# Lambda-mask attention with a gated feed-forward part: the first two 384-row halves computed the same way, each weight group used by both in turn

## The chip, the cores and the metric

One core of a Trainium2 chip. The metric is device microseconds (us) of one execution. Runs of the kernel before lie within 1.3% of each other (258.0 to 261.2 us, 35 runs of the fifth call). A run that is over 1.5% above the fastest of the same kernel is called slow here and left out of every ratio; medians take in all runs. A verdict is "faster" or "slower" from 2% on.

## The reference, cut to what matters

```python
# q, k, v: 4 batches, 8 heads, 768 rows, 64 columns, float32; n_global = 8, n_local = 96
scores = scale * np.matmul(q, k.transpose(0, 1, 3, 2))
rel = pos[:, None] - pos[None, :]
is_global = pos[None, :] < n_global
is_local = (rel >= 0) & (rel < n_local)
dist = np.where(is_global & ~is_local, n_local, np.abs(rel))
scores = scores - slopes[:, None, None] * dist          # one slope for each head
scores = np.where(is_global | is_local, scores, -1e9)
a = softmax(scores);  x = (a @ v), heads side by side: 3072 rows of 512
gate = np.maximum(x @ w_gate, 0.0);  val = x @ w_val    # 512 -> 1536
return (gate * val) @ w_out                             # 1536 -> 512
```

## The kernel before

Each batch is cut into two halves of 384 rows, eight in all, called half 0 to half 7. The attention of a half is made of small pieces that are laid among the feed-forward matmuls of the half before (`weave` places a piece by the share of the work done). Program order on each engine's queue is the order in which these lines are called.

The inputs of half 2 and later go this way: GpSimd casts k and q to bf16, the sync queue transposes them by DMA, and GpSimd copies the transposed keys into `kT`, whose key tiles overlap by the 8 global keys. Pieces of one half in this order:

```python
    def early_pieces(s):
        out = [(0.0, lambda p=p: piece_cast_k(s, p)) for p in range(HP)]     # GpSimd casts
        out += [(0.0, lambda n=n: piece_xk(s, n)) for n in range(NN)]        # sync: kN <- kc
        out += [(0.0, lambda p=p: piece_cast_q(s, p)) for p in range(HP)]    # GpSimd casts
        out += [(0.0, lambda n=n: piece_xq(s, n)) for n in range(NN)]        # sync: qT <- qz
        out += [(0.0, lambda p=p: piece_order(s, p)) for p in range(HP)]     # GpSimd: kT <- kN
        return out
```

v and the weights are loaded by GpSimd, cast to bf16 on the way; k and q by the sync queue. The 8 global rows of v are loaded once and copied six times within SBUF, by DMA on the sync queue:

```python
    def spread_v_globals(b, j0=1, j1=NT):
        for j in range(j0, j1):
            nc.sync.dma_start(out=v_dst(b, 0, NG, j), in_=v_dst(b, 0, NG, 0))
```

The start of the program (cut):

```python
    weave(f1_0, attention_pieces(1),                       # half 1's attention among half 0's gates and vals
          [(0.05 * h, lambda h=h: mask(h)) for h in range(H)])
    ...
    load_w(wo_sb, moe_w_out, 0, DM)                        # output weights, on GpSimd
    ...
    load_qk_after(2)
    load_v_half(2)
    weave(f1_1, spread(early_pieces(2), 0.0, 1.0))
    load_qk(3, 0, H)
    load_v_half(3)
    weave(f2_0 + f2_1, spread(attention_pieces(2), 0.0, 0.9), spread(early_pieces(3), 0.2, 0.7))
```

The softmax here doesn't subtract the row's maximum and nothing guards it: scores larger than these inputs give would overflow.

Of the kernel before, what the change touches and what calls it, by code (L numbers as in the profile page):

```python
# [8 lines left out]
FP32 = mybir.dt.float32  # L9
# [6 lines left out]
def kernel(  # L16
# [45 lines left out]
    banks_of_half[1] = [[by[1, 2], by[1, 5]], [by[1, 3], by[1, 6]], [by[1, 4]]]  # L62
    first_groups = [[by[0, 0], by[0, 1]], [by[0, 2], by[0, 3]]]

# [12 lines left out]
    first = ExitStack()  # L77
    P["es"] = first.enter_context(tc.tile_pool(name="es2", bufs=4))
    P["qk"] = first.enter_context(tc.tile_pool(name="qkps2", bufs=3, space=bass.MemoryType.PSUM))

    def other_pools():
        first.close()
        P["es"] = ctx.enter_context(tc.tile_pool(name="es", bufs=3, reuse_waits="tile"))
        P["qk"] = ctx.enter_context(tc.tile_pool(name="qkps", bufs=3, space=bass.MemoryType.PSUM,
                                                 reuse_waits="tile"))
        P["ff"] = ctx.enter_context(tc.tile_pool(name="ffps", bufs=3, space=bass.MemoryType.PSUM,
                                                 reuse_waits="tile"))
# [61 lines left out]
    def load_v_half(s):  # L149
        b, half = divmod(s, 2)  # L150
        if half == 0:
            load_v_globals(b)
            spread_v_globals(b)
        for j in range(4) if half == 0 else range(4, NT):
            load_v(b, j)
# [7 lines left out]

    def load_qk_after(s, by_pairs=False):

        qs_of[s] = stage.tile([128, H, NN * D], FP32, name="qs")
        ks_of[s] = stage.tile([128, H, NN * D], FP32, name="ks")
        step = 2 if by_pairs else H
        for t in (qs_of[s], ks_of[s]):
            nc.vector.memset(t[0:1, 0:H:step, 0:1], 0.0)  # L170
        for h in range(0, H, step):
            load_qk(s, h, h + step)
# [6 lines left out]
    nc.vector.memset(ones, 1.0)  # L179
    warm_ps = av_psum.tile([128, 512], FP32, name="av_ps")  # L180

    def warm(n):

        for _ in range(n):
            nc.tensor.matmul(warm_ps, lhsT=wo_sb[:, 0, 0:128], rhs=wo_sb[:, 0, :], start=True, stop=True)
# [43 lines left out]
    def piece_cast(s, p):  # L229
        qk = cast_pool.tile([128, 2, NN, 2, D], BF16, name="qk")  # L230
        cast_of[s, p] = qk
        for i, src in ((1, ks_of[s]), (0, qs_of[s])):
            copy = nc.gpsimd.tensor_copy
            if s == 0 and p < 3:
                copy = (nc.vector.tensor_copy, nc.scalar.copy, nc.scalar.copy)[p]
            copy(
                qk[:, i].rearrange("t n e d -> t e n d"),
                src[:, 2 * p : 2 * p + 2, :].rearrange("t e (n d) -> t e n d", n=NN))
# [20 lines left out]
    def piece_t(s, p):  # L259
# [5 lines left out]
        for i in range(2):  # L265
            for n in range(NN):
# [3 lines left out]
                                 start=(i == 0 and n == 0), stop=(i == 1 and n == NN - 1))  # L270
        if s == 0:
            nc.vector.tensor_copy(qTb[0][:, p, 0, :], tp[:, 0, :])
        else:
            qd = qTb[s % 2][:, p]
            nc.vector.tensor_copy(qd[0:64, 0, :], tp[0:64, 0, :])
            nc.vector.tensor_copy(qd[64:128, 1, :], tp[64:128, 0, :])
        put_keys(nc.vector.tensor_copy, nc.vector.tensor_copy, kt, tp[:, 1, :], half)
# [34 lines left out]

    def piece_bias(p, g):

        ps = P["qk"].tile([128, 2, 512], FP32, name="qk_ps")
        ps_of[p, g] = ps
        for e in range(2):
            c = 0
            for i, (j, a, w, m) in enumerate(first_groups[g]):
                nc.tensor.matmul(ps[:, e, c : c + NN * w], lhsT=sid[:, 2 * p + e],  # L320
                                 rhs=dd[:, 0 if j == 0 else 1, :, m : m + w],
                                 start=(i == 0), stop=False, skip_group_check=True)
                c += NN * w

    def piece_score(p, g):

        kt = kT[0][p]
        qd = qTb[0][:, p, 0, :].rearrange("d (n p) -> d n p", n=NN)
        group = first_groups[g]
        cols = sum(NN * w for _, _, w, _ in group)  # L330
        ps = ps_of[p, g]
        es = P["es"].tile([128, 2, cols], BF16, name=f"es{g}")
        c = 0
        for i, (j, a, w, m) in enumerate(group):
            for e in range(2):
# [3 lines left out]
                                 skip_group_check=True)  # L339
            es_of[0, p, j] = (es, c)  # L340
            c += NN * w
        nc.scalar.activation(es, ps[:, :, 0:cols], AF.Exp, bias=0.0, scale=scale)

# [58 lines left out]

    def piece_av_wide(p):

        s = 0
        todo = [t for group in first_groups for t in group]
        if p % 2 == 1:
            t = P["qk"].tile([128, 2, 512], FP32, name="qk_ps")
            av = [t[:, i] for i in range(2)]
        else:  # L410
            av = [av_psum.tile([128, 512], FP32, name="av_ps") for _ in range(2)]
# [19 lines left out]
    def attention_pieces(s):  # L431
        T = lambda p: [(0.34, lambda: piece_t(s, p))]
        QK = lambda p: [(0.18, lambda g=g: piece_qk(s, p, g)) for g in range(3)]
        AW = lambda p: [(0.58, lambda: piece_av_wide(p))]
        AV = lambda p: [(0.29, lambda e=e: piece_av(s, p, e)) for e in range(2)]
        C = lambda p: [(0.0, lambda: piece_cast(s, p))]
        BI = lambda p, *gs: [(0.2, lambda g=g: piece_bias(p, g)) for g in gs]
        SC = lambda p, *gs: [(0.2, lambda g=g: piece_score(p, g)) for g in gs]
        X = lambda *fs: [(0.0, f) for f in fs]
        if s == 0:  # L440
            return (C(0) + X(lambda: load_v_globals(0), lambda: load_v(0, 0)) + C(3)
                    + X(lambda: load_v(0, 1), lambda: load_v(0, 2), lambda: spread_v_globals(0, 1, 4),
                        lambda: load_v(0, 3), lambda: load_w_group(0))
                    + C(1) + T(0) + BI(0, 0, 1) + C(2) + T(1) + SC(0, 0, 1) + BI(1, 0) + SC(1, 0) + T(2)
                    + BI(1, 1) + SC(1, 1) + BI(2, 0) + T(3) + SC(2, 0) + BI(2, 1) + SC(2, 1)
                    + BI(3, 0) + SC(3, 0) + BI(3, 1) + SC(3, 1)
                    + AW(0) + X(lambda: load_qk_after(1, True)) + AW(1) + AW(2) + AW(3) + X(other_pools))
        if s == 1:
            at = lambda *ts: list(ts)
            C_ = lambda p: piece_cast(1, p)  # L450
            return ([(0.0, lambda: C_(0)), (0.0, lambda: C_(1)), (0.02, lambda: load_w_group(1)),
                     (0.04, lambda: C_(2)), (0.05, lambda: C_(3)), (0.07, lambda: load_w_group(2))]
                    + [(0.08, lambda j=j: fill_ones(nc.gpsimd, 0, j)) for j in range(NT)]
                    + [(t, lambda p=p: piece_t(1, p)) for p, t in enumerate((0.10, 0.14, 0.20, 0.26))]
                    + [(t, lambda p=p, g=g: piece_qk(1, p, g))
                       for p, ts in enumerate(((0.15, 0.18, 0.22), (0.26, 0.30, 0.34), (0.38, 0.42, 0.46),
                                               (0.54, 0.58, 0.62))) for g, t in enumerate(ts)]
                    + [(t, lambda p=p, e=e: piece_av(1, p, e))
                       for p, ts in enumerate(((0.37, 0.42), (0.52, 0.56), (0.66, 0.70), (0.81, 0.85)))
                       for e, t in enumerate(ts)])  # L460
        g = QK(3)
# [80 lines left out]
    for p in range(HP):  # L542
        nc.gpsimd.memset(qTb[1][64:128, p, 0, :].bitcast(mybir.dt.uint32), 0)
        nc.gpsimd.memset(qTb[1][0:64, p, 1, :].bitcast(mybir.dt.uint32), 0)

    f1_0, f2_0 = ffn_pieces(0)
    f1_1, f2_1 = ffn_pieces(1)
    weave(f1_0, attention_pieces(1),
          [(0.05 * h, lambda h=h: mask(h)) for h in range(H)])
    for p in range(HP):  # L550
        nc.gpsimd.memset(kT[1][p][:, 3, 32:128].bitcast(mybir.dt.uint32), 0)
        nc.gpsimd.memset(kT[1][p][:, 6, NG + 48 : 128].bitcast(mybir.dt.uint32), 0)
    nc.gpsimd.memset(vbuf[1][:, NT - 1, :].bitcast(mybir.dt.uint32), 0)
    for j in range(NT):
        fill_ones(nc.gpsimd, 1, j)
    load_w(wo_sb, moe_w_out, 0, DM)
    for i in range(2):
        nc.gpsimd.memset(qz[i].rearrange("t n p e z -> t (n p e z)").bitcast(mybir.dt.uint32), 0)
    load_qk_after(2)
    load_v_half(2)  # L560
    weave(f1_1, spread(early_pieces(2), 0.0, 1.0))
    load_qk(3, 0, H)
    load_v_half(3)
    weave(f2_0 + f2_1, spread(attention_pieces(2), 0.0, 0.9), spread(early_pieces(3), 0.2, 0.7))

# [45 lines left out]
```

## Time and profile before

| | before |
|---|---|
| time, median of 4 runs | 259.96 us (259.52 to 260.48) |
| profiled span | 258.3 us, granted clock 0.985 |
| TensorE busy | 238.5 us (92%) |
| TensorE idle from 17.45 to 90.44 us | 10.4 us (5.6 + 2.1 + 2.7 in the prediction's stretches) |

The prediction shows the page and TensorE's waits. What it did not look at closely, and what the result turned on, is the order on two DMA queues. The sync queue's timeline (start, length of issuing, line, what, count) and the piece of the chain of waits in which the last of these three transposes lands:

```profile
63.17 3.94 SPq L295 DMA_TRANSPOSE qT<-qz  x3
```

```profile
65.80 2.84 DMA qT<-qz
```

And GpSimd's:

```profile
37.42 1.04 POOL L158 DMA_DIRECT2D wo_sb<-in_moe_w_out_dram  x1
```

Half 2's three query transposes take 3.94 us to issue and the last lands 2.84 us after its issue began; TensorE waits 0.79 us for them:

```profile
68.77 0.53 PE L355 MATMUL qk_ps<-qT,kT 128*128 128x432 bf16 x2 [0.79 <-DMA qT<-qz]
```

The output weights (1536 KB, 12.9 us from issue to landing) are issued at 37.42 and are in the chip by about 50, long before those transposes. That order is an accident of where half 2's loads stood.

### The profile page before, as it was taken

The page shows a single profiled execution, that of the slowest core. Times are in us where ns is not written, and L with a number is a line of the kernel's source. Part 1 is how long each engine was busy: PE and PEld are TensorE (multiplying, and loading weights), DVE is VectorE, ACT ScalarE, POOL GpSimd, SP SyncE. Part 2 cuts the span into 40 slices and gives each one's busy share as a digit, 9 for nine tenths or more (in the row PEclk, how much of TensorE's full clock was granted, in tenths as well). Part 3 has the DMA queues.
Part 4 walks back from the last instruction along what each step waited for, and adds up shares of the span by engine and source line. Part 5 has one row for each costly group of instructions (what it writes and reads, how often), then busy time and mean ns, then how long its engine had stood idle before and what let it go on. Part 6 is the DMA issues. An engine that isn't in the chain of part 4 may idle for free.

```text
span 258.3 us, 4682 instructions
## 1 busy us (share of the span) xinstructions
PE 238.5 (92%) x1623; PEld 139.5 (54%) x1623; DVE 131.7 (51%) x333; ACT 159.3 (62%) x325; POOL 97.7 (38%) x244
## 2 busy tenths in 40 slices
PE   6754988999898899999999999999999999999994
PEld 2541645556454466655665566655665566556541
DVE  3521788644354467634675276625773457614410
ACT  5772689633376677756875577747774677643311
POOL 7791899015864706800644235600640000000000
PEclk9997799999999999999999999999999999999999
DMA  6999999994899993855681995927591200021012
GB/s 176 115 142 226 207 208 173 176 219 116 212 276 185 173 291 91 141 71 156 190 141 26 196 255 119 107 88 207 133 119 53 81 3 1 0 84 41 0 43 82
DMA packets 82695, 34.36 MB, mean 133 GB/s; under 512 B 58608, under 2 KB 79600, under 8 KB 82672
## 3 DMA queue, kind: packets, MB, share of 16 engines
q1 hardware_dynamic: 50816, 26.16, 38.8%
q0 software_dynamic: 31856, 7.91, 31.6%
q8 instruction: 13, 0.21, 0.3%
q14 instruction: 10, 0.08, 0.1%
HBM read 28.38 MB, written 6.29 MB: 134 GB/s over the span
## 4 chain that ended last, share of the span: by engine, by line
PE 65%; DMA 15%; SPq 5%; DVE 5%; ACT 5%; POOL 2%; issue 2%; DVEq 0%; ACTq 0%; POOLq 0%
PE ff_ps L497 21%; PE ff_ps L488 18%; PE ff_ps L478 17%; DMA qs<-in_q_dram 8%; PE av_ps L383 5%; PE qk_ps L355 4%; DVE xT L400 3%; DMA wv<-in_moe_w_val_dram 3%; SPq L291 2%; SPq L122 2%; DMA vbuf<-in_v_dram 2%; ACT rcp L397 1%; ACT lnd L392 1%; DVE ht L490 1%; DMA kN<-kc 1%
## 5 line engine op out<-in xcount | busy, mean ns | idle before, releaser
L488 PE MATMUL ff_ps<-xT,wv 128*128 128x384 bf16 x384 | 79.4, 330 | 4.6 <-DMA wv<-in_moe_w_val_dram 3.8
L478 PE MATMUL ff_ps<-xT,wg 128*128 128x384 bf16 x384 | 79.0, 328 | 3.7 <-DMA wg<-in_moe_w_gate_dram 2.9
L481 ACT ACTIVATE grelu<-ff_ps 128x384 bf16<-128x384 f32 x96 | 47.0, 490 | 38.2 <-DVE ht L490 18.2
L490 DVE TENSOR_TENSOR ht<-ff_ps,grelu 128x384 bf16<-128x384 f32 x96 | 53.1, 555 | 29.5 <-PE ff_ps L488 25.1
L497 PE MATMUL ff_ps<-wo_sb,ht 128*128 128x512 bf16 x288 | 67.3, 379 | 0.0
L400 DVE TENSOR_TENSOR xT<-av_ps,rcp 64x384 bf16<-64x384 f32 x56 | 31.1, 556 | 46.5 <-ACT rcp L397 42.1
L358 ACT ACTIVATE es<-qk_ps 128x432 bf16<-128x432 f32 (+2 forms) x84 | 44.2, 532 | 14.1 <-PE qk_ps L355 12.6
L367 DVE TENSOR_TENSOR es<-es,m_all 128x432 bf16<-128x432 bf16 (+6 forms) x128 | 39.2, 337 | 26.9 <-ACT es L358 26.3
L488 PEld LDWEIGHTS <-wv 128*128 128x128 bf16 x384 | 36.5, 98 | 27.8 <-DMA wv<-in_moe_w_val_dram 4.3
L478 PEld LDWEIGHTS <-wg 128*128 128x128 bf16 x384 | 36.5, 98 | 26.5 <-DMA wg<-in_moe_w_gate_dram 3.3
L497 PEld LDWEIGHTS <-ht 128*128 128x128 bf16 x288 | 27.0, 97 | 28.1
L280 POOL CAST kc<-ks 128x384 bf16<-128x384 f32 x24 | 12.1, 549 | 60.7 <-DMA ks<-in_k_dram 60.7
L392 ACT ACTIVATE lnd<-av_ps 64x384 f32<-64x384 f32 x56 | 27.2, 485 | 12.8 <-PE av_ps L383 12.0
L355 PE MATMUL qk_ps<-qT,kT 128*128 128x432 bf16 (+6 forms) x128 | 28.8, 285 | 0.9 <-DMA qT<-qz 0.8
L502 ACT COPY osb<-ff_ps 128x512 f32<-128x512 f32 x24 | 14.1, 586 | 24.2 <-PE ff_ps L497 21.7
L383 PEld LDWEIGHTS <-vbuf 128*128 128x128 bf16 x256 | 21.0, 98 | 11.0 <-issue 2.7
L383 PE MATMUL av_ps<-es,vbuf 128*128 128x216 bf16 (+5 forms) x256 | 25.1, 225 | 1.7 <-DVE xT L400 1.7
L141 POOL DMA_DIRECT2D vbuf<-in_v_dram x28 | 24.4, 882 | 0.5 <-issue 0.4
L355 PEld LDWEIGHTS <-kT 128*128 128x128 bf16 x128 | 12.4, 98 | 10.7 <-issue 2.3
L288 POOL CAST qz<-qs 128x192 bf16<-128x192 f32 x48 | 14.4, 351 | 4.0 <-DMA qs<-in_q_dram 4.0
L397 ACT ACTIVATE rcp<-lnd 128x384 f32<-128x384 f32 x28 | 14.6, 522 | 0.9
L251 POOL COPY kT<-kN 128x360 bf16<-128x360 bf16 x12 | 6.6, 551 | 5.9 <-DMA kN<-kc 5.9
(75 smaller groups left out, 108.2 us busy)
## 6 DMA issues: line engine op xcount, KB each, us to landing
out_dram<-osb SPq DMA_DIRECT2D x24, 256.0 KB
ks<-in_k_dram SPq DMA_DIRECT2D x6, 768.0 KB
qs<-in_q_dram SPq DMA_DIRECT2D x6, 768.0 KB
vbuf<-in_v_dram POOLq DMA_DIRECT2D x24, 120.0 KB, 4.8
ks<-in_k_dram SPq DMA_DIRECT2D x8, 192.0 KB
qs<-in_q_dram SPq DMA_DIRECT2D x8, 192.0 KB
wg<-in_moe_w_gate_dram POOLq DMA_DIRECT2D x3, 512.0 KB, 7.4
wv<-in_moe_w_val_dram POOLq DMA_DIRECT2D x3, 512.0 KB, 10.2
```

Source lines behind the costliest of these rows:

```text
L141: nc.gpsimd.dma_start(out=v_dst(b, NG + r0, NG + r0 + n, j), in_=v[b, :, KT * j + r0 : KT * j + r0 + n, :].rearrange("h p d -> p h d"))
L355: nc.tensor.matmul(ps[:, c : c + n_], lhsT=kt[:, j, :], rhs=qd[:, :, :, a : a + w], start=True, stop=True)
L358: nc.scalar.activation(es[:, 0:cols], ps[:, 0:cols], AF.Exp, bias=0.0, scale=scale)
L367: nc.vector.tensor_mul(e4, e4, mk)
L383: nc.tensor.matmul(av3[:, :, a : a + w], lhsT=vb[:, j, z0 : z0 + 128], rhs=es[:, c : c + NN * w].rearrange("k (n p) -> k n p", n=NN), star ...
L392: nc.scalar.activation(ln[o0 : o0 + 64], av[d0 : d0 + 64, 0:QH], AF.Ln, bias=0.0, scale=1.0)
L400: nc.vector.tensor_tensor(xT_of[s][r, p, :], av_of[s, p, e_][r, 0:QH], rc[r], op=ALU.mult)
L478: nc.tensor.matmul(psg[:, 0:QH], lhsT=w_of(wg, dc, fc), rhs=xT[:, dc, :], start=(dc == 0), stop=(dc == N_DC - 1))
L481: nc.scalar.activation(gr, psg[:, 0:QH], AF.Relu, bias=0.0, scale=1.0)
L488: nc.tensor.matmul(psv[:, 0:QH], lhsT=w_of(wv, dc, fc), rhs=xT[:, dc, :], start=(dc == 0), stop=(dc == N_DC - 1))
L490: nc.vector.tensor_tensor(ht[:, fc, :], psv[:, 0:QH], st["gr"], op=ALU.mult)
L497: nc.tensor.matmul(ps2, lhsT=ht[:, fc, n * 128 : (n + 1) * 128], rhs=wo_sb[:, fc, :], start=(fc == 0), stop=(fc == N_FC - 1))
```

## The change

Its intent: half 1 gets its distance bias from TensorE (a matmul into the scores' buffer) and its scores in row halves, as half 0 has them, so that VectorE is spared the masks; half 1's attention comes in one burst after weight group 0 of half 0; then each of the three groups of gate and val weights is used by half 0 and half 1 in turn, which gives the later groups more time to arrive. The casts of half 0's last pair of heads go from GpSimd to VectorE, so that v and the weights are issued earlier; eight matmuls without use ("warm") bridge a gap at the first gate. Half 2's inputs are fetched some 20 us earlier. The diff, cut to its core:

```diff
-    weave(f1_0, attention_pieces(1),
-          [(0.05 * h, lambda h=h: mask(h)) for h in range(H)])
+    weave(f1_0[G[0]], spread(attention_pieces(1), 0.75, 3.0))
+    other_pools()
+    load_w_group(2)
+    load_qk_after(2, nc.gpsimd)
 ...
+    load_v_globals(1)
+    e2 = early_pieces(2)
+    for _, f in e2[:-HP]:               # casts and transposes of half 2
+        f()
     load_w(wo_sb, moe_w_out, 0, DM)     # now BEHIND half 2's casts on GpSimd
-    load_qk_after(2)
+    for _, f in e2[-HP:]:               # key copies of half 2
+        f()
+    spread_v_globals(1)
     load_v_half(2)
-    weave(f1_1, spread(early_pieces(2), 0.0, 1.0))
-    load_qk(3, 0, H)
-    load_v_half(3)
-    weave(f2_0 + f2_1, spread(attention_pieces(2), 0.0, 0.9), spread(early_pieces(3), 0.2, 0.7))
+    weave(f1_1[G[0]] + f1_0[G[1]] + f1_1[G[1]],
+          [(0.1 + 0.1 * h, lambda h=h: mask(h)) for h in range(H)])
+    weave(f1_0[G[2]] + f1_1[G[2]] + f2_0 + f2_1,
+          [(0.4, lambda: load_qk(3, 0, H)), (0.4, lambda: load_v_half(3))],
+          spread(attention_pieces(2), 0.15, 0.8), spread(early_pieces(3), 0.5, 0.9),
+          [(0.02 * j, lambda j=j: fill_ones(nc.vector, 0, j)) for j in range(NT)])
 ... (in half 0)
-                    + AW(0) + X(lambda: load_qk_after(1, True)) + AW(1) + AW(2) + AW(3) + X(other_pools))
+                    + AW(0) + X(lambda: load_qk_after(1, nc.vector, True)) + AW(1) + AW(2) + AW(3) + X(second_pools, lambda: warm(8)))
```

Nothing in the stated intent asks for the output weights to move. The line kept its place among its neighbours, and half 2's casts and transposes moved ahead of it.

## The prediction

> **What bounds the kernel now.** I read first the busy shares and the 40 slices of the page, for the engine that is full and the stretch in which it is not.
>
> ```profile
> PE 238.5 (92%) x1623; PEld 139.5 (54%) x1623; DVE 131.7 (51%) x333; ACT 159.3 (62%) x325; POOL 97.7 (38%) x244
> PE   6754988999898899999999999999999999999994
> ...
> DMA  6999999994899993855681995927591200021012
> ```
>
> TensorE is full from the fifteenth slice (90 us) to the end. Then I cut the trace into stretches and read the busy time of each engine in each (columns: stretch, length, then PE, PEld, DVE, ACT and POOL with their counts, granted clock, DMA share, GB/s).
>
> ```profile
> 17.45:29.10 11.65, 6.06 (x30) 3.48 (x31) 3.94 (x10) 4.04 (x9) 5.66 (x15) 0.71 1.29 215
> 29.10:51.58 22.48, 20.36 (x157) 12.70 (x155) 18.17 (x54) 18.67 (x40) 15.87 (x37) 1.00 1.35 186
> 51.58:90.44 38.86, 36.18 (x218) 19.91 (x218) 16.95 (x39) 20.12 (x42) 21.92 (x56) 1.00 1.03 197
> 90.44:231.16 140.72, 140.10 (x934) 82.95 (x932) 79.19 (x192) 96.40 (x194) 39.77 (x107) 1.00 0.56 117
> ```
>
> After 90.44 TensorE idles 0.6 us in 141. The change leaves that code alone, so its whole worth lies before 90 us: 5.6 us idle in the first stretch, 2.1 in the second, 2.7 in the third. The clock adds to it. One-microsecond stretches show 0.50 from 22 to 28.6 us, and from 23.87 on TensorE is busy all the time, so some 4.9 us of work ran at half speed: 2.4 us lost. Together 12.8 us could be had at the very most. What ended the idle times stands in TensorE's timeline (start, length, line, what, count, idle before it and its releaser).
>
> ```profile
> 20.34 0.82 PE L478 MATMUL ff_ps<-xT,wg 128*128 128x384 bf16 x4 [2.90 <-DMA wg<-in_moe_w_gate_dram]
> 23.87 1.46 PE L488 MATMUL ff_ps<-xT,wv 128*128 128x384 bf16 x4 [2.70 <-DMA wv<-in_moe_w_val_dram]
> ...
> 35.95 0.82 PE L488 MATMUL ff_ps<-xT,wv 128*128 128x384 bf16 x4 [1.05 <-DMA wv<-in_moe_w_val_dram]
> ...
> 40.37 0.47 PE L383 MATMUL av_ps<-es,vbuf 128*128 128x72 bf16 x5 [0.74 <-DVE xT L400]
> ```
>
> So the feed-forward part starts on the weights' DMA, and four matmuls of 384 columns took 1.46 us at half clock against 0.82. Why the weights are late, the GpSimd timeline and two windows of one microsecond show.
>
> ```profile
> 8.34 0.51 POOL L236 CAST qk<-ks 128x384 bf16<-128x384 f32 x1 [1.12 <-DMA ks<-in_k_dram]
> 9.11 0.51 POOL L236 CAST qk<-qs 128x384 bf16<-128x384 f32 x1 [0.27 <-DMA qs<-in_q_dram]
> 9.56 2.70 POOL L141 DMA_DIRECT2D vbuf<-in_v_dram  x3
> 12.26 0.79 POOL L158 DMA_DIRECT2D wg<-in_moe_w_gate_dram  x1
> ```
>
> ```profile
> 9.00:10.00 1.00, 1.00 (x18) 0.69 (x18) 0.23 (x1) 1.00 (x3) 0.89 (x2) 1.00 0.66 42
> 10.00:11.00 1.00, 0.89 (x14) 0.71 (x10) 1.00 (x5) 0.57 (x2) 1.00 (x2) 1.00 0.04 7
> ```
>
> GpSimd waits for a slice of k, casts it, and only then issues v and the weights; meanwhile the DMA engines run dry (7 GB/s).
>
> **What the Trainium skill says.** "TensorE: Matmul & The Clock Gate", part 1: the clock falls to half after an idle window of about 3.4 us and returns after a busy one, the window running free. The trace agrees in length: half clock lasted 6.6 us, about two windows; but the window before the fall was not quite empty, it held 0.65 us of matmuls. The same page, "Back-to-back issue gap": N/2.4 + 2.5 ns, so 162.5 ns for 384 columns; the chain of waits after 90 us steps by 0.65 us for four, which agrees. "TensorEngine Tiling (Array Packing)", "Key Properties": different tiles run in parallel, but changing the mode drains the array. In the first half's attention four row-half matmuls of 216 columns took 0.29 us (12.65 to 12.94), where two side by side twice would be 0.18: parallel, with a toll.
>
> **The change, part by part.** I call the 384-row halves 0, 1, 2; one feed-forward item is four matmuls, 0.65 us; a half has 24 such items plus 7.8 us for its output (36 matmuls at 0.216).
>
> Earlier loads. The two casts move to VectorE (0.36 us each), so three v loads and the first weights are issued 2.4 us sooner (wg at 9.9 instead of 12.26) into the dry stretch. The attention of half 0 is held by ScalarE and would gain only 1 us (last normalised tile at 18.8 instead of 19.8). First gate at about 18.9, first val at 21.4 instead of 23.87: minus 2.4 us.
>
> Eight warming matmuls (1.7 us at full clock) fill about 16.7 to 18.4. The longest gap then is near 1.8 us before the first val, where before there were 2.9 and 2.7 us. If that holds the clock: minus 2.4 us. I give this 60%, as the window's phase is chance.
>
> Half 1's attention is no longer spread among 24 items but comes as one burst after group 0 of half 0. On TensorE a pair of heads costs: transpose 0.34; bias 1392 columns in 10 matmuls, about 0.80 (0.75 in half 0 for 1200); scores in row halves 0.53; sums and values in column halves 0.66. That is 2.33, for four pairs 9.3 us. Before it was 20.36 - 85 x 0.1625 = 6.5 in the second stretch plus 0.6 for two transposes, 7.1. Plus 2.2 us of TensorE work. The masks' multiplications (20 at 0.2 to 0.4 us) and half the normalising on VectorE go; these lay beside TensorE.
>
> What paces the burst is ScalarE. From the groups by shape: 864 columns 890 ns, 336 columns 446 ns, hence 0.84 ns a column; 816 and 576 columns cost 0.85 and 0.65. Four pairs: 4 x 1.50 + 4 x (0.48 logarithm + 0.52 reciprocal) = 10.0 us in a row. First exponential at about 27.7 (group 0 done at 26.5, transposes and VectorE's copies 1.2 us), and the emission order (two score buffers, two output buffers, each freed by the step before) adds about 1 us of bubbles: half 1's last tile at 39. TensorE idles 3.1 us in the burst (11.7 less 8.6), against the 2.1 of the second stretch before. Plus 1.0.
>
> Only two feed-forward buffers during group 0: a val waits for the multiply of the val before, some 0.15 us three times. Plus 0.4.
>
> Groups in turn. After the burst 24 items run bare on loaded weights (group 1 is needed at 44, not at 36), then 16 items and both outputs, 26 us, take half 2's attention from 0.15 to 0.8. Its inputs are fetched from about 30 us instead of 52, so the waits for q and the late normalisation (0.79, 0.97, 0.16, 0.77 us) go. What remains is the transposed q of half 3, queued behind outputs on the sync queue: I leave 0.7. Minus 2.0.
>
> Sum: -2.4 - 2.4 + 2.2 + 1.0 + 0.4 - 2.0 = -3.2 us with the clock held, -0.8 without. The last stages are the same. Working out the burst step by step gave about -4, so 256.2 to 257 with the clock held.
>
> **The rivals.** (1) The burst eats the gain: TensorE gets 2.2 us more work and nothing to fill ScalarE's 10 us with. If each hand-over costs 0.2 us more, half 1 ends at 41 to 42 and the time is 259 to 260. For it: ScalarE was 5.0 of 5.0 us busy from 30 to 35 with less in a row. Against: VectorE loses its masks, which had held it full there. (2) The DMA was saturated anyway: from 20 to 28 us it moved 190 to 260 GB/s, so earlier issue might only reorder. Then the first val stays at 23, the clock falls, and the time is about 259. Against: the dry stretch at 10 us is free capacity. (3) Better than I think: the burst's idle time shrinks to nothing, the weights come 3 us earlier, no wait remains before 90 us; then some 252. (4) A fetch that now comes too late (output weights, issued after half 2's casts) stops the outputs: 261 or more. It has some 20 us of slack, so this is unlikely.
>
> **Range and chances.** Between the sum with clock held (257.0) and the step-by-step working (256.0), with some weight on (3) because the constants look tuned, and on (1) and (2): 256.3. Range 252.8 to 259.6. Faster by over 2% needs under 255.0, that is, nearly all parts working: 0.30. Slower by over 2% needs (4): 0.03.
>
> **What would show it right or wrong.** The granted clock at 1.00 from 18 to 30 us; wg and wv read first at about 19 and 21.4; no second wait for weights; half 1's first gate of group 0 at about 38 to 39; TensorE idle about 3 us in the burst with ScalarE nearly full; under 1 us idle between the burst and the third half's first gate at about 85 to 86. It is wrong if the clock falls all the same, if wv is not read before 23, or if the burst lasts beyond 41.

## The result, and the profile after

| | before | after |
|---|---|---|
| median (range) | 259.96 us (259.52 to 260.48), 4 runs | 273.40 us (270.04 to 274.98), 4 runs |
| fast runs | all four, mean 259.98 | 272.63 and 270.04, mean 271.34 |
| profiled span, clock | 258.3 us, 0.985 | 270.7 us, 0.967 |

The ratio of the fast runs is 1.044, 95% interval 1.035 to 1.053: slower. Ratios here are the mean time of one kernel's fast runs over that of the other's of the same rounds, so not quite the ratio of the medians quoted. The loss to be explained is that of the fast runs, 11.4 us; the median is 13.4 only because two of four runs are slow. The prediction was 256.3 us; it was wrong, in direction too.

The page of the changed kernel (busy tenths of TensorE and granted clock, 40 slices of 6.8 us each):

```profile
PE   6969979990999959999999999999999999999994
...
PEclk9979999997699986999999999999999999999999
```

The tenth slice of TensorE shows 0: around 61 to 68 us it does nothing at all. In that slice and the next the clock drops, and there is a second, smaller dent of both five slices on. TensorE's timeline names the two waits (in brackets the idle time before the instruction, and what ended it):

```profile
68.30 0.52 PE L358 MATMUL qk_ps<-qT,kT 128*128 128x432 bf16 x1 [8.05 <-DMA qT<-qz]
...
100.07 0.56 PE L358 MATMUL qk_ps<-qT,kT 128*128 128x144 bf16 x2 [3.25 <-DMA qT<-qz]
```

These are the first scores of half 2 and of half 3, each waiting for its transposed q. Each wait is also paid a second time: the clock falls to 0.50, and work runs at half speed until it returns. Windows of one microsecond show 0.50 from 65.0 to 71.8 us (3.5 us of it with matmuls, so about 1.75 lost) and from 99.1 to 105.9 (5.85 us of it busy, about 2.9 lost); a window with a mean of 0.55 has fallen for nine tenths of its length. Three of the windows (length, busy time of PE, PEld, DVE, ACT and POOL, clock, DMA share, GB/s):

```profile
66.00:67.00 1.00, 0.00 (x0) 0.00 (x0) 0.00 (x0) 0.00 (x0) 0.00 (x0) 0.50 1.70 156
...
71.00:72.00 1.00, 1.00 (x7) 0.49 (x6) 0.38 (x1) 0.25 (x2) 0.00 (x0) 0.60 1.15 347
...
99.00:100.00 1.00, 0.00 (x0) 0.00 (x0) 0.00 (x0) 0.00 (x0) 0.00 (x0) 0.55 1.53 281
```

From 66 to 67 us no engine works, and the DMA moves 156 GB/s. 8.05 + 1.75 + 3.25 + 2.9 = 16.0 us; less the waits of about 2.7 us that the kernel before had in that stretch and the 0.4 us by which the changed kernel was ahead at half 1's first val (reckoned at the end), that is 12.9, against a difference of the two profiled spans of 12.4. So the loss is in these two places, within half a microsecond, and elsewhere the change is worth little.

Why does q come late? The sync queue, to be held against the one line of before:

```profile
47.99 13.90 SPq L298 DMA_TRANSPOSE qT<-qz  x3
61.99 4.37 SPq L146 DMA_DIRECT2D vbuf<-vbuf  x6
66.40 0.45 SPq L131 DMA_DIRECT2D ks<-in_k_dram  x1
...
81.19 3.81 SPq L496 DMA_DIRECT2D out_dram<-osb  x2
...
91.59 3.99 SPq L298 DMA_TRANSPOSE qT<-qz  x3
```

The same three transposes took 13.90 us to issue in place of 3.94, and held up everything behind them: value rows, and half 3's keys and queries, loaded at 66.4. Half 3's own query transposes then stand behind outputs of half 0 and half 1 and are issued at 91.59. In the chain of waits half 2's last transpose lands 10.23 us after its issue, not 2.84, and half 3's last 5.65 us after:

```profile
57.94 10.23 DMA qT<-qz
...
94.28 5.65 DMA qT<-qz
```

Half 3's last transpose has half 4's value loads beside it (issued by GpSimd from 93.23 us on). At 2.84 us it would have landed by 97.1, and of the second wait some 0.4 us would be left (an estimate from these lines). So that wait may be made by the place on the queue or by the company at that place.

And GpSimd, shortly before and during this:

```profile
46.71 1.03 POOL L167 DMA_DIRECT2D wo_sb<-in_moe_w_out_dram  x1
...
55.22 6.11 POOL L150 DMA_DIRECT2D vbuf<-in_v_dram  x7
```

Two suspects share the DMA engines with half 2's transposes: the output weights (1536 KB, issued at 46.71, landing after 15.2 us, at about 62) and seven value loads of 120 KB. The value loads can't have begun the delay: at the pace of before, 5.47 us from the first issue to the last landing (63.17 to 68.64), the transposes would have landed by 53.5, before the first value load was issued. They can have drawn it out, as the last transpose lands 6 us after the output weights.

The head of the program changed too:

```profile
17.01 0.20 PE L420 MATMUL av_ps<-es,vbuf 128*64 128x24 bf16 x2 [2.32 <-DMA vbuf<-vbuf]
...
22.14 0.81 PE L471 MATMUL ff_ps<-xT,wg 128*128 128x384 bf16 x4
22.79 0.81 PE L481 MATMUL ff_ps<-xT,wv 128*128 128x384 bf16 x4
```

The first half's values wait 2.32 us for the copied global rows, and the first gate runs at 22.14, later than before (20.34); but the first val runs at 22.79, not 23.87, and at full clock. One trace says little here, though: nine kernels of this study (the changed one, `e1_wo_first` to `e5_half3_first`, `e9_order_warm`, `e11_two_moves`, `e13_keys_after_scores`) have the same code up to this point, and in their traces the first val runs anywhere from 20.84 to 24.82 us (the middle one 22.88) and half 1's first gate from 37.67 to 41.65 (39.14 to 41.65 within the first call). What makes this spread is not known. The two traces of the old head have the first val at 23.87 and 24.04.

### The profile page after: what moved, and what is told of

The parts are those of the page before. It is cut to its first block, busy times and chain, and to the rows that moved or that the text cites. A ratio compares the mean times of both kernels' runs of the same rounds, so it can differ in the third digit from the quotient of the medians.

```text
span 270.7 us, 4853 instructions
## 1 busy us (share of the span) xinstructions
PE 248.3 (92%) x1731; PEld 146.3 (54%) x1731; DVE 124.3 (46%) x312; ACT 158.0 (58%) x317; POOL 92.7 (34%) x229
## 4 chain that ended last, share of the span: by engine, by line
PE 71%; DMA 10%; SPq 6%; ACT 4%; DVE 4%; POOL 2%; issue 2%; POOLq 0%; DVEq 0%; ACTq 0%
PE ff_ps L481 20%; PE ff_ps L490 19%; PE ff_ps L471 19%; DMA qT<-qz 6%; PE qk_ps L358 5%; PE av_ps L386 4%; SPq L298 4%; DMA vbuf<-vbuf 2%; DVE xT L403 2%; DMA vbuf<-in_v_dram 1%; DVE ht L483 1%; ACT es L345 1%; SPq L294 1%; DMA kN<-kc 1%; PE qk_ps L420 1%
## 5 line engine op out<-in xcount | busy, mean ns | idle before, releaser
L361 ACT ACTIVATE es<-qk_ps 128x432 bf16<-128x432 f32 (+2 forms) x72 | 37.9, 529 | 23.9 <-PE qk_ps L358 22.3
L370 DVE TENSOR_TENSOR es<-es,m_all 128x432 bf16<-128x432 bf16 (+5 forms) x108 | 32.4, 328 | 41.2 <-ACT es L361 40.7
L403 DVE TENSOR_TENSOR xT<-av_ps,rcp 64x384 bf16<-64x384 f32 x48 | 26.7, 555 | 45.3 <-ACT rcp L400 40.7
L358 PE MATMUL qk_ps<-qT,kT 128*128 128x432 bf16 (+5 forms) x108 | 26.0, 298 | 11.3 <-DMA qT<-qz 11.3
L283 POOL CAST kc<-ks 128x384 bf16<-128x384 f32 x24 | 12.4, 557 | 68.3 <-DMA ks<-in_k_dram 68.3
L395 ACT ACTIVATE lnd<-av_ps 64x384 f32<-64x384 f32 x48 | 23.3, 485 | 10.5 <-PE av_ps L386 9.8
L386 PEld LDWEIGHTS <-vbuf 128*128 128x128 bf16 x216 | 18.1, 98 | 7.8 <-issue 0.5
L358 PEld LDWEIGHTS <-kT 128*128 128x128 bf16 x108 | 10.8, 101 | 20.1 <-issue 13.1
L386 PE MATMUL av_ps<-es,vbuf 128*128 128x216 bf16 (+4 forms) x216 | 21.3, 226 | 0.2 <-DVE xT L403 0.2
L345 ACT ACTIVATE es<-qk_ps 128x864 bf16<-128x864 f32 (+3 forms) x16 | 10.7, 706 | 4.2 <-PE qk_ps L340 4.2
L400 ACT ACTIVATE rcp<-lnd 128x384 f32<-128x384 f32 x24 | 12.5, 523 | 0.8
```

What stands on the lines that cost most here:

```text
L358: nc.tensor.matmul(ps[:, c : c + n_], lhsT=kt[:, j, :], rhs=qd[:, :, :, a : a + w], start=True, stop=True)
L361: nc.scalar.activation(es[:, 0:cols], ps[:, 0:cols], AF.Exp, bias=0.0, scale=scale)
L370: nc.vector.tensor_mul(e4, e4, mk)
L386: nc.tensor.matmul(av3[:, :, a : a + w], lhsT=vb[:, j, z0 : z0 + 128], rhs=es[:, c : c + NN * w].rearrange("k (n p) -> k n p", n=NN), star ...
L395: nc.scalar.activation(ln[o0 : o0 + 64], av[d0 : d0 + 64, 0:QH], AF.Ln, bias=0.0, scale=1.0)
L403: nc.vector.tensor_tensor(xT_of[s][r, p, :], av_of[s, p, e_][r, 0:QH], rc[r], op=ALU.mult)
```

## The experiments

Fourteen kernels, in the order in which they ran, as diffs against the changed kernel ("after") if nothing else is said. All gave correct results.

**First call: which load slows the transposes?** Before: 259.69 us in the same call.

`e1_wo_first`, the output weights' load put ahead of half 2's casts on GpSimd:

```diff
+    load_w(wo_sb, moe_w_out, 0, DM)
     load_v_globals(1)
     e2 = early_pieces(2)
     for _, f in e2[:-HP]:
         f()
-    load_w(wo_sb, moe_w_out, 0, DM)
```

> The changed kernel with one line moved: the output weights' load is issued by GpSimd before half 2's casts (at about 36 us) instead of after them (46.7 us). Theory A: the three transposes of q took 13.9 us to issue and the last landed 10.2 us after its issue because this load shared the DMA engines with them. Then they issue in about 4 us, land within 3 us, the 8.05 us stall of TensorE before half 2's first scores falls to under 1 us, the clock stays full from 60 to 72 us, and the second stall (3.25 us at 97) shrinks as half 3's loads are no longer late: about 257 to 260 us. Theory B: the seven v loads of small packets issued at 55 us made it. Then the stall stays near 8 us and the time near 272.

Measured: 261.19 us (260.43 to 265.73, one of four slow), ratio to before 1.006 [1.000, 1.012], a little above the 257 to 260 expected. Its sync queue:

```profile
53.80 4.24 SPq L298 DMA_TRANSPOSE qT<-qz  x3
```

And its TensorE:

```profile
90.28 0.36 PE L358 MATMUL qk_ps<-qT,kT 128*128 128x144 bf16 x2 [3.34 <-DMA qT<-qz]
```

One moved line brought back some 10 us (mean of the fast runs 260.94, from 271.34): issuing takes 4.24 us again and the wait at half 2 is gone. q itself arrives later, as its load now shares with the output weights (GpSimd's casts of q wait 6.17 us, until 51.37), and still it is in time. The second wait, at half 3, stays; that its loads were no longer late did not help it.

`e2_v_first`, half 2's value loads put ahead, the output weights left: 

```diff
     load_v_globals(1)
+    load_v_half(2)
 ...
     spread_v_globals(1)
-    load_v_half(2)
```

> The changed kernel with half 2's four v loads issued before half 2's casts (about 36 us), the output weights' load left after the casts. Theory A (output weights contend): the stall before half 2's first scores stays at 5 us or more, the time at 268 or more. Theory B (v loads contend): the stall goes, 257 to 260 us. If both share it, something between, with the last transpose landing sooner than 68 us but the second one's issue still at several us.

Measured: 271.63 us, ratio 1.047 [1.042, 1.052]; waits of 8.36 and 3.18 us.

```profile
49.66 11.46 SPq L298 DMA_TRANSPOSE qT<-qz  x3
```

With half 2's four value loads out of the way the wait is as long as before (issuing 11.46 us in place of 13.90, the last landing 15.64 us after its issue), so these four don't make it. Half 3's three value loads are still issued at 55.23 us, so a share of theirs in the slow landing is not excluded; as in the changed kernel they come too late to have begun it (49.66 + 5.47 = 55.1).

`e3_both_first`, both moves at once:

> The changed kernel with both loads issued before half 2's casts, in the order of the kernel before. Under A and B alike the transposes run alone as they did in the kernel before: issue about 4 us, landing about 3 us, no stall over 1 us before half 2's first scores, 256 to 259 us. If the stall stays, neither load is its cause, and it is something that the transposes do by themselves at this place (theory C).

Measured: 266.02 us, ratio 1.024 [1.016, 1.031]. Issuing took 5.61 us, but q was cast only from 54.4 on, the first wait is 1.91 us and the second still 3.17. Too much ahead of q is no good either: the loads in front of it delay q itself. Its head also waited longer (4.4 us for the copied rows), but the moved loads are issued only at 37.8 us, so that is the spread of the head and no work of the edit.

**Second call: dose, the second wait, the warm matmuls, the earlier loads.** Before: 259.55 us.

`e4_half_wo`, one half of the output weights ahead of the casts and the other behind:

```diff
+    nc.gpsimd.dma_start(out=wo_sb[:, 0:6], in_=moe_w_out[0:768, :].rearrange("(c p) f -> p c f", p=128))
     load_v_globals(1)
 ...
-    load_w(wo_sb, moe_w_out, 0, DM)
+    nc.gpsimd.dma_start(out=wo_sb[:, 6:12], in_=moe_w_out[768:1536, :].rearrange("(c p) f -> p c f", p=128))
```

> Dose: the changed kernel with the first half of the output weights' load issued early, as in e1, and the second half left behind half 2's casts. If the transposes of q are slow because they share the DMA engines with the bytes of this load, the q transposes should take about half as long to issue as in the changed kernel (6 to 9 us instead of 13.9), the stall of TensorE before half 2's first scores should fall from 8 us to between 0 and 4 us, and the time to some 261 to 267 us. If it is the mere presence of any load behind the casts (an ordering or a semaphore), the stall stays at 7 us or more and the time near 272.

Measured: 272.97 us, ratio 1.050 [1.045, 1.055]: a miss. Half the load beside the transposes did not give half the loss. The early half delayed q (cast at 48.34 in place of 44.38), the late half was issued at 50.67 just as the transposes began, and these took 10.22 us to issue; the wait was 6.82 us. So the loss doesn't go with the load's size alone; where it lies to the transposes counts. How the two share the engines in detail stays open.

`e5_half3_first`, `e1_wo_first` and further half 3's loads and transposes ahead of half 1's outputs on the sync queue:

```diff
     load_v_globals(1)            # behind the output weights, as in e1_wo_first
+    spread_v_globals(1)
 ...
-    spread_v_globals(1)
+    load_qk(3, 0, H)
     load_v_half(2)
+    load_v_half(3)
 ...
-          [(0.4, lambda: load_qk(3, 0, H)), (0.4, lambda: load_v_half(3))],
-          spread(attention_pieces(2), 0.15, 0.8), spread(early_pieces(3), 0.5, 0.9),
+          spread(attention_pieces(2), 0.15, 0.8), spread(early_pieces(3), 0.42, 0.5),
```

> e1 with the sync queue reordered: half 2's copies of the global v rows before its transposes, half 3's q and k loads straight after them, and half 3's transposes placed between 0.42 and 0.5 of the stage, ahead of all but the first output. Theory: the second stall (3.34 us at 90 us in e1, and 3 us of half clock after it) is half 3's transposes queued behind four outputs. Then it goes, and the time falls from 261 to about 256 to 257.5, 1 to 1.5% under the kernel before. Rival: half 3's transposes are slow from half 4's v loads at the same time; then a stall of 2 us or more stays, and 259 to 260.

Measured: 268.42 us, ratio 1.032 [1.025, 1.038]. The wait at half 3 is gone. This edit moves half 3's loads too; `e11_two_moves` below moves only its casts, transposes and key copies, and the wait goes as well. But I had put the copies of the global value rows ahead of the transposes, and they wait for a load that now stands behind the output weights:

```profile
52.38 4.63 SPq L146 DMA_DIRECT2D vbuf<-vbuf  x6
...
61.13 3.95 SPq L298 DMA_TRANSPOSE qT<-qz  x3
```

The transposes are fast (3.95 us) but late, and TensorE waits 4.63 us. A wait of my own making.

`e6_no_warm`, the same without the eight warm matmuls:

```diff
-                    ... + AW(3) + X(second_pools, lambda: warm(8)))
+                    ... + AW(3) + X(second_pools))
```

> e5 without the eight warming matmuls. My prediction gave them 2.4 us at 60%. If they hold the clock, without them the feed-forward part starts at half clock and the time is 1.5 to 2.5 us over e5. If the clock comes back by the attention's matmuls alone, or the start is held by something else, the difference is under 0.7 us.

Measured: 267.54 us, ratio to before 1.029 [1.024, 1.034], nothing to tell from `e5_half3_first`. But this pair can't price the warm matmuls. In the trace without them half 1's first gate runs at 38.11 us, with them at 41.48, and half 2's first score comes at the same time all the same, for it waits for q in both:

```profile
66.74 0.34 PE L358 MATMUL qk_ps<-qT,kT 128*128 128x432 bf16 x1 [4.63 <-DMA qT<-qz]
66.76 0.52 PE L358 MATMUL qk_ps<-qT,kT 128*128 128x432 bf16 x1 [8.02 <-DMA qT<-qz]
```

(The first line is `e5_half3_first`, the second `e6_no_warm`.) Whatever the head gains or loses, this wait takes up. The clock is at 0.50 from 16.0 to 22.9 us with them and from 17.4 to 20.8 without, and at 1.00 after it until that wait.

`e7_late_loads`, `e5_half3_first` with the cast of the last pair of heads of half 0 back on GpSimd, ahead of the v and weight loads, as in the kernel before:

```diff
-            return (C(0) + X(lambda: load_v_globals(0), lambda: load_v(0, 0), lambda: load_v(0, 1),
+            return (C(0) + X(lambda: load_v_globals(0), lambda: load_v(0, 0)) + C(3) + X(lambda: load_v(0, 1),
```

> e5 with the cast of the last pair of heads of half 0 back on GpSimd ahead of three v loads and the first weights, as in the kernel before. My prediction gave the earlier issue 2.4 us. In the trace of the changed kernel half 0's values waited 2.3 us for the copies of the global v rows, which share the DMA engines with the loads now issued earlier. If the earlier issue gains what the first val shows (1.1 us), e7 is about 1 us over e5; if the copies' delay eats it, the two are within 0.5 us; if my term was right, 2 us or more.

Measured: 269.89 us, ratio 1.038 [1.032, 1.044]; the first val waits for its weights 2.05 us and runs at 23.87. The total is 1.5 us above that of `e5_half3_first`, but this does not price the head either: half 1's first gate runs at 40.71 us, earlier than the 41.48 there. The time is lost at half 2, whose query transposes are issued at 63.63 in place of 61.13; TensorE waits 7.90 us for them. What the trace does show is that TensorE's last waits at the head are here for the value loads (1.31 and 0.58 us) and not for the copied rows.

**Third call: the orders mended, and the cause tried on the kernel before.** Before: 260.34 us.

`e8_order_no_warm` and `e9_order_warm`: `e5_half3_first` with the global rows' load ahead of the output weights, and the copies between half 2's key and query transposes; without and with the warm matmuls.

```diff
     load_v_globals(1)
+    load_w(wo_sb, moe_w_out, 0, DM)
     e2 = early_pieces(2)
-    for _, f in e2[:-HP]:
+    for _, f in e2[: HP + NN]:
         f()
-    load_w(wo_sb, moe_w_out, 0, DM)
+    spread_v_globals(1)
+    for _, f in e2[HP + NN : -HP]:
+        f()
+    load_qk(3, 0, H)
     for _, f in e2[-HP:]:
         f()
-    spread_v_globals(1)
     load_v_half(2)
+    load_v_half(3)
```

> The changed kernel without the eight warm matmuls, with the output weights' load issued first of all on GpSimd after the second batch's global value rows (as in e1_wo_first), the copies of those rows on the sync queue between half 2's key and query transposes, half 3's query and key loads right behind half 2's query transposes on the sync queue, and half 3's transposes ahead of half 1's late outputs. Theory (the time of the change went into two waits for query transposes, the first made by the output weights' load running beside them, the second by their place behind other work on the sync queue; the rest of the change is worth about what was predicted): no wait of TensorE for query transposes above 1.5 us, query transposes' issue about 4 us for half 2 and half 3, first half's attention ends at about 38 us, total 253 to 257 us, 1 to 3% below the kernel before. Rival (the two halves together cost TensorE more than the removed work, or there is a third wait that the two hid): waits gone but total 260 us or more. Second rival (every ordering moves the wait: the transfers of this stretch are simply more than the queues carry in the time): a wait of 3 us or more at half 2's or half 3's scores, total 262 to 268 us.

> As e8_order_no_warm but with the eight warm matmuls kept. If the warm matmuls hold the clock, this is 1 to 3 us faster than e8_order_no_warm; if, as e6_no_warm showed, the clock comes back without them, it is 0 to 2 us slower, with the first gate 2 to 3 us later.

Measured: 263.95 us, ratio 1.014 [1.007, 1.020], and 264.09 us, ratio 1.015 [1.010, 1.019]: the range of the second rival (each order moves the wait), not of the theory. The totals with and without the warm matmuls don't differ. In the profile of `e8_order_no_warm` half 2 still waits 2.89 us for q; in that of `e9_order_warm` no wait for q above 0.2 us is left, but a new one took its place:

```profile
68.12 0.27 PE L386 MATMUL av_ps<-es,vbuf 128*128 128x216 bf16 x1 [1.78 <-DMA vbuf<-in_v_dram]
```

Three such waits for half 2's values, 3.1 us in all, with half clock from 68.6 to 75.4 us. Half 3's k and q, now issued at 58.88, run beside half 2's value loads, issued at 58.94.

`e10_before_wo_late`, the kernel *before* with its output weights' load behind half 2's query casts:

```diff
-    load_w(wo_sb, moe_w_out, 0, DM)
 ...
-    weave(f1_1, spread(early_pieces(2), 0.0, 1.0))
+    e2 = early_pieces(2)
+    e2.insert(2 * HP + NN, (0.0, lambda: load_w(wo_sb, moe_w_out, 0, DM)))
+    weave(f1_1, spread(e2, 0.0, 1.0))
```

> The kernel before with one line moved: the output weights' load is issued on GpSimd only behind half 2's query casts, where the changed kernel has it, so that it runs beside half 2's query transposes. Theory (the load beside them slows the transposes): their issue on the sync queue grows from 3.94 us to 8 us or more and their landing from 2.84 us to 5 us or more, and a wait for them of some us appears at half 2's scores; total 2 to 8 us over before. Rival (the changed kernel's stall comes from its other traffic or from its ordering, the output weights only being a part of it): issue stays below 5.5 us and the total within 1 us of before.

Measured: 274.06 us, ratio 1.050 [1.043, 1.056]. GpSimd's line, the sync queue's and the chain's:

```profile
62.05 1.05 POOL L158 DMA_DIRECT2D wo_sb<-in_moe_w_out_dram  x1
```

```profile
62.88 12.88 SPq L295 DMA_TRANSPOSE qT<-qz  x3
```

```profile
71.56 10.21 DMA qT<-qz
```

Set these beside the changed kernel's 13.90 and 10.23, and the 3.94 and 2.84 of before: in a kernel that has nothing else of the change, one moved load makes the same slow transposes. (The total, well above the 2 to 8 us expected, is not all theirs: TensorE also waits 10.15 us for the output weights themselves, and then 2.48 for q.)

**Fourth call: only what is needed.** Before: 260.07 us over all its runs.

`e11_two_moves`, `e1_wo_first` and one number pair more, so that half 3's casts and transposes stand ahead of the outputs and its loads stay where they are:

```diff
-          spread(attention_pieces(2), 0.15, 0.8), spread(early_pieces(3), 0.5, 0.9),
+          spread(attention_pieces(2), 0.15, 0.8), spread(early_pieces(3), 0.42, 0.5),
```

> e1_wo_first (the output weights' load put ahead of half 2's key and query casts, 261.2 us) with one more move and nothing else: half 3's casts and transposes at 0.42 to 0.50 of the second stretch of work in place of 0.5 to 0.9, so that they stand ahead of half 1's outputs on the sync queue. Half 3's loads stay where they are, so half 2's values aren't disturbed as in e8_order_no_warm and e9_order_warm. Theory (two waits for query transposes were the whole loss, and each has one cause: the load beside them, the place in the queue): both waits are gone, so the 3.3 us of TensorE's idle time and about 1.7 us of low clock that e1_wo_first still had go too, total 255 to 258 us, 1 to 2% below the kernel before. Rival (the stretch holds more transfers than its time carries, so each removed wait comes back in another place, as in e9_order_warm): some other wait of 2 us or more between 60 and 100 us, total 260 us or more.

Measured: 261.11 us median of 22 runs, five of them slow; ratio 1.003 [1.001, 1.005]. Both old waits are nearly gone (1.75 us at half 2, none at half 3), and a third appeared, as the rival had said; the trace explains it:

```profile
80.24 0.22 PE L358 MATMUL qk_ps<-qT,kT 128*128 128x48 bf16 x1 [2.36 <-POOL kT L264]
```

This is the last score of half 2. It reads key tile 3, whose tail half 3's keys fill. With the pieces moved up, GpSimd's copies for half 3 come *before* this score in program order, so it must wait for them.

`e12_two_moves_no_warm`, the same without the warm matmuls:

> e11_two_moves without the eight warm matmuls. By e6_no_warm against e5_half3_first and e8_order_no_warm against e9_order_warm: within 1 us of e11_two_moves, if anything 0.5 us less, the clock being 0.50 for one window near 17 to 21 us and 1.00 after it with or without them.

Measured: 264.63 us median of 6 runs, from 259.94 to 266.48; only two count as fast (mean 261.27, against 260.87 for the fast runs of `e11_two_moves`), so there is no interval. Its trace is the one hint that the warm matmuls may do something. The first val with and without them:

```profile
20.84 0.81 PE L481 MATMUL ff_ps<-xT,wv 128*128 128x384 bf16 x4
20.92 1.48 PE L481 MATMUL ff_ps<-xT,wv 128*128 128x384 bf16 x4
```

Without them the clock is at 0.50 from 17.4 to 24.3 us; in the trace of `e11_two_moves` it is at 1.00 all that time. But it fell here before the place where the warm matmuls would stand, and it is one trace of each: open.

**Fifth call: the third wait, and the one at the head.** Before: 259.70 us.

`e13_keys_after_scores`, `e11_two_moves` with half 3's key copies put back behind half 2's scores:

```diff
+    e3 = early_pieces(3)
 ...
-          spread(attention_pieces(2), 0.15, 0.8), spread(early_pieces(3), 0.42, 0.5),
+          spread(attention_pieces(2), 0.15, 0.8), spread(e3[:-HP], 0.42, 0.5), spread(e3[-HP:], 0.82, 0.9),
```

> e11_two_moves (261.1 us) with half 3's four groups of key copies on GpSimd put back behind half 2's last scores in the program (0.82 to 0.90), the casts and transposes staying early. In e11_two_moves the last score of half 2 reads a key tile whose tail half 3's key copies fill, and it waited 2.36 us for them (77.9 to 80.24), after which the clock was 0.50 for about 3.4 us (0.83 from 80 to 90): some 4 us. Theory: that is the last of the loss, so no wait of TensorE above 2 us from 40 to 100 us, clock 1.00 there, total 256.5 to 258.5 us, 0.6 to 1.4% below the kernel before. Rival (each removed wait comes back elsewhere): a wait of 2 us or more at half 3's scores or values, total 260 us or more.

Measured: 259.93 us median of 22 runs, six of them slow; ratio 0.999 [0.997, 1.001]: the same as before to a thousandth, and 11.8 us below the changed kernel (means of the fast runs, 259.49 and 271.34). Leaving out the slow runs favours it: of the 87 runs of the kernel before none is slow, and with its six slow ones this kernel's mean is 260.63, 0.9 us above that of before (259.77). What the slow runs do differently was not looked into.

```profile
54.80 4.67 SPq L298 DMA_TRANSPOSE qT<-qz  x3
...
78.58 3.94 SPq L298 DMA_TRANSPOSE qT<-qz  x3
```

From 40 to 100 us TensorE is busy 57.38 of 60 us (before 56.66, after 48.40), at a clock of 1.00, and its longest wait is 0.72 us. The mechanism came as expected, the total 1.4 us above the range that I gave.

`e14_rows_on_vector`, the same with the first three copies of the global value rows made by VectorE:

```diff
-                             lambda: load_v(0, 2), lambda: spread_v_globals(0, 1, 4),
+                             lambda: load_v(0, 2),
 ...
+    def copy_v_globals():
+        for j in range(1, 4):
+            nc.vector.tensor_copy(v_dst(0, 0, NG, j), v_dst(0, 0, NG, 0))
 ...
-                    + AW(0) + ...
+                    + X(copy_v_globals) + AW(0) + ...
```

> e13_keys_after_scores, with the first batch's three copies of the global value rows made by VectorE ahead of the first values, in place of DMA on the sync queue (VectorE is idle there for 4.4 us). The values of the first pair then wait for no copy: theory (the copies land late because they share the DMA engines with the loads that the change moved ahead): the wait of 2.2 us goes, the first half's attention ends about 2 us earlier, 1.5 to 3 us less than e13_keys_after_scores. Rival (the values themselves land only a little earlier, or the weights do): a wait for the value loads or for the weights takes its place, less than 1 us gained.

Measured: 258.58 us median of 14 runs, two of them slow; ratio 0.996 [0.993, 0.999], the only kernel of this study whose interval lies below the one before, by 0.4%; it is 0.7 us below `e13_keys_after_scores` (means of the fast runs), which is the rival's range and not the theory's. The wait for copies is gone, and the weights' takes its place:

```profile
13.89 0.20 PE L424 MATMUL av_ps<-es,vbuf 128*64 128x24 bf16 x2 [0.27 <-DMA vbuf<-in_v_dram]
...
18.06 0.81 PE L475 MATMUL ff_ps<-xT,wg 128*128 128x384 bf16 x4
21.23 0.82 PE L485 MATMUL ff_ps<-xT,wv 128*128 128x384 bf16 x4 [2.35 <-DMA wv<-in_moe_w_val_dram]
```

The first gate is 4 us earlier than in the changed kernel, the first val only 1.6. The wait for the weights is followed by half clock from 22.4 to 25.8, and half 1's first gate comes at 39.32, only 0.3 us earlier than in the changed kernel.

## Why the prediction was wrong

**The step that failed** is "Its inputs are fetched from about 30 us instead of 52, so the waits for q and the late normalisation ... go. ... Minus 2.0." This term came out at about plus 13 in the profiled run (16.0 us of waits and half clock, less the 2.7 us of waits that went). Fetched earlier does not mean there earlier. The earlier fetch, as it was ordered on GpSimd, put half 2's query transposes beside the output weights' load. `e1_wo_first` and `e10_before_wo_late` show this cause from both sides: take the load away from the transposes and some 10 of the 11.4 us come back; bring it to them in the kernel before, and they show the same 13 and 10 us. The value loads, the other suspect, didn't begin the delay, and `e2_v_first` clears four of the seven; whether the other three draw it out stays open.

**Rival (4)**, the one that pointed at this load, was put aside with "It has some 20 us of slack". That asked only whether the output weights would be late for the outputs. In the changed kernel no wait for them stands in TensorE's list. The harm was done to what ran *beside* them. The chance of 3% for slower came from this.

**"What remains is the transposed q of half 3 ... I leave 0.7"** had the right place and a size far too small: 3.25 us and half clock after it. Moving half 3's transposes ahead of the outputs removes it, as `e11_two_moves` shows, which moves nothing else but `e1_wo_first`'s line; `e5_half3_first`, `e9_order_warm` and `e13_keys_after_scores` have none of it either. But moved ahead they also have less of half 4's value loads beside them, and no run separates the late place from the slow landing there (5.65 us).

**Earlier loads, minus 2.4.** Half right, as far as the spread of the head lets one see. Read off the first val the gain was 1.1 us (22.79 for 23.87; from 20.84 to 24.82 in the nine traces of this head), and `e7_late_loads` can't price it. The prediction's own times, first gate at 18.9 and first val at 21.4, turn up nearly exactly in `e14_rows_on_vector` (18.06 and 21.23). So the weights did come as predicted; what was missed are the copies of 8 KB that ran beside the earlier loads: TensorE waited 2.32 us for them. The dry stretch of the DMA engines was filled (share from 0.04 to 1.82 at 10 to 11 us), and something small that had used it was slowed.

**Warming matmuls, minus 2.4, at 60%.** The clock was held at 1.00 where before it had been 0.50, from 22 us on; but it fell earlier, from 17.2 to 20.6, ahead of the warm matmuls (20.25), while TensorE was busy. Half of these 3.4 us is lost, about 1.7, against 2.4 before, so at most some 0.7 us of this term was gained. (The prediction read half clock before as ending at 28.6; the window from 28 to 29, at 0.59, puts it at 28.8, which its 4.9 us fit.) Whether the warm matmuls had a part in the clock's return is not shown: in `e6_no_warm` and `e8_order_no_warm` it is back at 20.8 without them, in `e12_two_moves_no_warm` only at 24.3.

**The burst.** Length right: from 27.15, the start of the burst (one val of group 0 still stands in it), to the end of half 1's wait at 40.43 there are 13.28 us, of which TensorE idles 1.85 (predicted "about 3"). Half 1's first gate was predicted "at about 38 to 39"; it is late by some 2 us, and the head lost about as much (first val 22.79, predicted 21.4; first gate 22.14, predicted 18.9).

**The sum, once the waits are gone.** `e13_keys_after_scores` is the change without its accidents. It is done with half 1's first gate at 41.01 us, with 16 items of half 0 (10.4 us) still to do that the kernel before has behind it there, so it is where that kernel would be at 51.4; that one starts half 1's first val at 51.58. So it is ahead by about 0.2 us (the changed kernel, at 40.75, by 0.4), where the terms up to there promised 1.2; and the smaller waits between 40 and 100 us cost 2.2 us where before it was 2.7 from 51 to 90. Together 0.7 us, and the profiled spans differ by 0.7 (257.6 and 258.3); the ratio of all the fast runs says 0.1%. The intended parts are worth 0 to 1 us, not 3.2: most of the first gain was held up at the head, and of the "minus 2.0" only 0.5 is to be had.

## What to carry to other kernels

When a change moves work to an earlier time, list what it will run *beside* there, queue by queue, and what was behind it in line and is now in front; a load that has slack itself can still take it from a transpose that has none. A query with a wait of 0.8 us in the old profile is a warning that this path has no slack at all. Before pricing an edit by the total, look whether a later wait takes up what it gains, as in `e6_no_warm`. And when a large change loses, try first to put single lines back into their old order: here one line was some 10 of 11.4 us, and three moves all of it.

## What the Trainium skill lacked or had wrong

- "DMA: Bandwidth & Descriptors" says under "Queues, rings and completion order" that each DMA engine goes round the queues that have work for it, a packet at a time. Sharing of that kind would fit what is seen here (no trace shows the order of the packets), but no page says what it costs a DMA transpose to run beside a casting load: the issue of three grew from 3.94 to 13.90 us (12.88 in the kernel before with the load moved), and the last one's landing from 2.84 to 10.23 us (10.21).
- The same page gives under "Latency and other measured facts" 261 GB/s for DMA transposes of a non-contiguous form, measured on one kernel, and no figure for a mix; from 61 to 68 us, with transposes, value loads and the 8 KB copies in flight, all queues together moved 120 to 156 GB/s.
- No page has the small copy beside large loads: copies of 8 KB within SBUF, issued from 8.85 us on, let TensorE wait until 17.01 us; three VectorE copies in their place took that wait away.
- "TensorE: Matmul & The Clock Gate", part 1: the table has the half clock "after ≥1 idle window (~3.4µs)". The wait of 8.05 us fits. But at half 3 the clock fell at 99.1 us, 2.3 us after the last matmul, and the 3.4 us before the fall held 1.1 us of matmuls; in the kernel before, counted the same way, the 3.4 us ahead of the fall (18.6 to 22.0) held 0.8 us (the prediction's 0.65 for the same four matmuls). So a window need not be empty for the clock to fall.
